# Two accumulating chains in PSUM instead of a separate addition per product, neighbouring sets interleaved, and no split weight unit kept in DRAM

## The chip, the cores and the metric

The kernel runs on one core of one Trainium2 chip. The metric is the time of one execution in microseconds (us), as the device measures it. Five engines work side by side, each through its own queue of instructions in order: TensorE (PE in the profile, with its weight loads as PEld), VectorE (DVE), ScalarE (ACT), GpSimd (POOL, unused here) and SyncE (SP, which issues all DMAs). TensorE writes its results to PSUM, which has eight banks; DVE and ACT read them from there.

## The reference, cut to what matters

```
scores = 1/sqrt(64) * q @ k.T - log(448)            # 4 batches, 12 heads, 448 rows, head size 64
x = (sigmoid(scores) @ v), heads side by side       # [1792, 768]
h = x @ w_in;  g = s * relu(h)**2 + b;  x = g @ w_out          # layer 0: 768 -> 2048 -> 768
h = x @ w_in2; g = max(h,0) + alpha * min(h,0); out = g @ w_out2   # layer 1, the same sizes
```

All is in float32. The weights arrive as 64-bit floats and are made into 32-bit ones on the chip.

## The kernel before, in words

**Attention** comes first: 84 units of QK products, a sigmoid on ACT, and products with V. **Then eight phases** follow, each 504 matmuls: layer 0 and layer 1 (m), each in two halves of the tokens (g), each half an "in" phase (times w_in) and an "out" phase (times w_out). The order is in(m,g), out(m,g) for (0,0), (0,1), (1,0), (1,1).

**Seven products.** Each phase multiplies 2x2 blocks with seven products M1 to M7 in place of eight. The sums of weight blocks that they need (S1 to S4) are made by `quad`, which loads 64-bit weights (tile `r`), turns them into 32-bit ones on ACT (line 303) and DVE (306, 311), forms the sums (324) and stores seven blocks to DRAM (`w0in`, `w0out`, `w1in`, `w1out`; line 342). A phase later reads these back in units of eight 128x128 blocks into `raw` (two buffers).

**Splits.** Each float32 operand is split into a high and a low part: ACT casts (line 397), DVE subtracts (line 400). Weight units go to `ring` (three buffers; in the first phase `rinq`, four smaller buffers over the same memory, filled straight from `quad`'s blocks), the "in" operand to `xo`, the "out" operand to `gb`. One weight block costs three matmuls (lines 491 to 493).

**In phase.** Eight sets (`mp`), one after the other. A product is 9 matmuls, a set 63. The results of a set are four blocks of `g`, which then go through the nonlinearity (lines 534, 535, 538 in layer 0; 553, 555, 558 in layer 1). `IN_ORDER` sets the order in a set. M1 is copied from its bank by ACT (502); M5, M6, M7, M4 and M3 are each added to a sum in SBUF by DVE (512, 520); M2 goes on top of M1 in M1's bank and is copied.

**Out phase.** Seven products one after the other, each for three output parts `k` with 24 matmuls each (one weight unit). The additions are made in the same way, and results are stored by SP (617). While a product runs, `prepare` makes the operand of the next one; under the last product the next phase's operand is loaded and split as well.

**Kept units.** In out(0,0) the split units from number `FROM` = 10 on (11 of 21) are stored to DRAM (`s0out`), and out(0,1) loads them instead of splitting them again.

**Order of the instructions.** All work is recorded in `Plan`, with an estimated duration each. `Plan.place` then fixes each engine's order: the PE keeps its recorded order, and every other engine takes the work that could start first, and of equals the most urgent one. The chip runs the queues so made; the estimates only set the order.

Of the kernel before, what the change touches and what calls it, by code (L numbers as in the profile page):

```python
# [16 lines left out]
P = 128  # L17
# [4 lines left out]
ROUNDS = 3  # L22
EARLY = 7
FROM = 10
# [5 lines left out]
IN_ORDER = ["M1", "M5", "M6", "M2", "M4", "M7", "M3"]  # L30
OUT_ORDER = ["M1", "M5", "M2", "M6", "M7", "M4", "M3"]
LEFT = {"M1": "A11", "M2": "A12", "M3": "S4", "M4": "A22", "M5": "S1", "M6": "S2", "M7": "S3"}
CHUNKS = [(0, 3), (3, 6), (6, 8)]


class Plan:
# [25 lines left out]
    def order(self):  # L62
# [10 lines left out]
        for _ in range(ROUNDS):  # L73
            late = [0.0] * n
            for i in range(n - 1, -1, -1):
                dur, lat = self.ops[i][1:3]
                x = min((late[s] for s in succ[i]), default=t + 50) - dur - lat
                late[i] = min(x, goal[i]) if i in goal else x
            done, at = self.place(succ, late, list(goal))
            goal = {i: at[i] for i in goal}  # L80
        return done

    def place(self, succ, late, pe):
# [10 lines left out]
        while len(done) < n:  # L94
# [29 lines left out]
            for s in succ[i]:  # L124
                est[s] = max(est[s], end + (lat if self.ops[s][0] != eng else 0.0))
# [30 lines left out]
def tile_kernel(  # L156
# [83 lines left out]
    ps = psp.tile([P, 8, 512], F32, name="ps")  # L240

# [3 lines left out]
    def act_t(n, psum=False):  # L245
        return (0.146 if psum else 0.183) + 0.844e-3 * n

    def dve_t(n, psum=False):
        return 0.155 + 1.037e-3 * n

    def dve2_t(n):
        return 0.16 + 0.53e-3 * n
# [23 lines left out]
    def quad(m, kind, k, c, place=0):  # L276

        QUAD = QUADS[place]
        order = IN_ORDER if kind == "in" else OUT_ORDER
# [53 lines left out]
        if kind == "in":  # L333
            dst = d[:, 7 * k * WQ : 7 * (k + 1) * WQ]
            src = sb(QUAD, 7 * n)
            wrote = [("d", m, kind, 7 * KH * k + i) for i in range(7 * KH)]
        else:
            dst = d.rearrange("p (i m n) -> p i m n", i=7, m=NDP)[:, :, k, c0 * P : c1 * P]
            src = q
            wrote = [("d", m, kind, (i * NDP + k) * 8 + j) for i in range(7) for j in range(c0, c1)]  # L340
        add(
            "SP", dma_t(7 * n), lambda: nc.sync.dma_start(out=dst, in_=src),
# [11 lines left out]
    def entry(at, n, ring_=RING):  # L354
        dst = ring_[n_unit[0] % len(ring_)]
        n_unit[0] += 1
        for j in range(n // P):
            ring[at // P + j] = (dst + j * P, dst + (n + j * P))
        return dst

    def unit(m, kind, i, g):
        at, n = i * UNIT, UNIT
        dst = entry(at, n)
# [23 lines left out]
    def direct(mp, place):  # L387

        for b0, b1 in ((0, 2), (2, 4), (4, 6), (6, 7)):
            n = (b1 - b0) * WQ  # L390
            dst = entry((7 * mp + b0) * WQ, n, RING4)
            split(dst, dst + n, QUADS[place] + b0 * WQ, n)
            yield
# [48 lines left out]
    def make_x(par, raw):  # L442
# [6 lines left out]
        def less(o, x, y):  # L449

            for t, a, e in x if len(x) > 1 else y:
# [10 lines left out]
        less(p[0], p[0], p[2])  # L462
# [63 lines left out]
    def nonlinear(m, par, mp, ps_):  # L526
# [4 lines left out]
        if m == 0:  # L531
            n = len(ps_) * S
            h, c = at(ps_)
            add("ACT", act_t(n), lambda: nc.scalar.activation(h, h, AF.Relu), c, c)
            add("ACT", act_t(n), lambda: nc.scalar.activation(h, h, AF.Square), c, c)
            add(
                "ACT", act_t(n) + 0.19,
                lambda: nc.scalar.activation(h, h, AF.Identity, bias=b_t, scale=s_t),
                c + [("sc",)] + [("bc",)], c,
            )  # L540
            return
        for row in range(2):
            some = [p for p in ps_ if p // 2 == row]
            if not some:
                continue
            n = len(some) * S
            h, c = at(some)
            ct = cells(NEG, n)
            t = sb(NEG, n).rearrange("p (b n) -> p b n", n=S)
# [3 lines left out]
                lambda t=t, h=h: nc.scalar.activation(t, h, AF.Relu, scale=-1.0), c, ct,  # L553
            )
            add("ACT", act_t(n), lambda h=h: nc.scalar.activation(h, h, AF.Relu), c, c)
# [7 lines left out]

    def in_phase(m, g, par):
        made = 0
        get = None
        for mp in range(NMP):
            k0 = 4 * (mp % 2)
            a, c, bb, e = k0, k0 + 1, k0 + 2, k0 + 3
            to = {"M1": a, "M2": a, "M5": c, "M4": c, "M6": bb, "M7": bb, "M3": e}  # L570
            second = {"M2", "M4", "M7"}
            if m == g == 0:
                get = direct(mp, 1 - mp % 2)
            for i, x in enumerate(IN_ORDER):
                terms = []
                for kc in range(KH):
                    n = (mp * 7 + i) * KH + kc
                    while (m or g) and made <= n // 8:
                        unit(m, "in", made, g)
                        made += 1  # L580
                    if m == g == 0 and i % 2 == 0 and kc == 0:
                        next(get)
                    xo = X[par][i]
                    terms.append((*ring[n], xo + kc * S, xo + XB + kc * S))
                mm_group(to[x], terms, x not in second, True, x in second)
                if x == "M1":
                    t = tmp()
                    pcopy(t, a)
                elif x == "M5":
                    s_ = tmp()  # L590
                    padd(s_, c, t)
                    free(t)
                elif x == "M6":
                    q = tmp()
                    padd(q, bb, s_)
                elif x == "M2":
# [344 lines left out]
```

## Time and profile before

| | us |
|---|---|
| three runs, median (lowest to highest) | 975.98 (974.36 to 978.29) |
| the profiled execution's own time | 972.68 |
| its span, first to last instruction | 970.9 |
| PE busy / DVE busy / ACT busy | 954.9 / 761.7 / 619.4 |

The profiled execution lies 3.3 us below the median. A busy PE is no proof of a full pace, since matmul records overlap; a stall shows as a longer step from one matmul's start to the next.

### The profile page before, as it was taken

Reading aid. Unit: us, or ns where it says so; the run is one execution under the profiler, and the core shown is the slowest. Engines: PE = TensorE matmul, PEld = TensorE weight load, DVE = VectorE, ACT = ScalarE, POOL = GpSimd, SP = SyncE. Lnnn points to the kernel's source line nnn. Section 1 sums busy time; section 2 is a strip of 40 time slices with the busy share of each in tenths; the row PEclk is TensorE's granted clock in tenths of the full one; section 3 lists DMA queues with packets and bytes.
Section 4 is the critical chain, followed back from the end, with each engine's and each line's share of the span. In section 5 each row is a group of like instructions: output and inputs, shape, how many; then the busy total and the mean of one; then the engine's idle time right before and its main releaser. Section 6 shows DMA issues by size and latency. Waiting matters only on the chain. (4 is left out here: it accounts for less than half of the span.)

```text
span 970.9 us, 13854 instructions
## 1 busy us (share of the span) xinstructions
PE 954.9 (98%) x5424; PEld 815.0 (84%) x5424; DVE 761.7 (78%) x905; ACT 619.4 (64%) x678; POOL 0.2 (0%) x4
## 2 busy tenths in 40 slices
PE   9999999998999999999999999997999999999998
PEld 4334459997999999999999999997999999999997
DVE  3547678888987987889988788989989666689862
ACT  7989966779864557879644366667545455576440
POOL 0000000000000000000000000000000000000000
PEclk9999999999999999999999999998999999999999
DMA  9999986685559998897489987775544443333441
GB/s 325 368 330 340 336 302 257 224 298 199 161 166 390 338 337 303 310 352 249 139 306 353 353 297 258 250 235 190 161 127 155 127 119 104 110 102 109 141 145 66
DMA packets 69618, 228.98 MB, mean 236 GB/s; under 512 B 6577, under 2 KB 30897, under 8 KB 64689
## 3 DMA queue, kind: packets, MB, share of 16 engines
q1 hardware_dynamic: 69552, 228.10, 67.9%
q8 instruction: 42, 0.69, 0.3%
q14 instruction: 24, 0.19, 0.0%
HBM read 158.74 MB, written 69.34 MB: 235 GB/s over the span
## 5 line engine op out<-in xcount | busy, mean ns | idle before, releaser
L491 PE MATMUL ps<-gb,ring 128*128 128x448 f32 x672 | 247.4, 368 | 6.8 <-DVE gb L400 5.2
L493 PE MATMUL ps<-gb,ring 128*128 128x448 f32 x672 | 247.0, 368 | 1.7 <-DVE ring L400 1.7
L492 PE MATMUL ps<-gb,ring 128*128 128x448 f32 x672 | 246.9, 367 | 0.0
L397 ACT CAST ring<-raw 128x1024 fp32r<-128x1024 f32 x136 | 142.3, 1048 | 147.1 <-PE ps L492 120.6
L400 DVE TENSOR_TENSOR ring<-raw,ring 128x1024 fp32r<-128x1024 f32 x136 | 165.7, 1220 | 24.0 <-ACT ring L397 23.4
L491 PE MATMUL ps<-xo,ring 128*128 128x448 f32 x504 | 184.1, 365 | 0.0
L493 PE MATMUL ps<-xo,ring 128*128 128x448 f32 x504 | 184.1, 365 | 0.0
L492 PE MATMUL ps<-xo,ring 128*128 128x448 f32 x504 | 184.1, 365 | 0.0
L491 PEld LDWEIGHTS ps<-gb,ring 128*128 128x128 f32 x672 | 127.3, 189 | 18.5 <-DVE gb L400 6.6
L493 PEld LDWEIGHTS ps<-gb,ring 128*128 128x128 f32 x672 | 127.2, 189 | 12.3 <-DVE ring L400 2.0
L492 PEld LDWEIGHTS ps<-gb,ring 128*128 128x128 f32 x672 | 127.2, 189 | 10.1
L400 DVE TENSOR_TENSOR gb<-g,gb 128x1344 fp32r<-128x1344 f32 (+1 forms) x84 | 116.8, 1398 | 15.9 <-ACT gb L397 9.1
L512 DVE TENSOR_TENSOR tmp<-ps,tmp 128x448 f32<-128x448 f32 x124 | 76.8, 622 | 61.2 <-PE ps L493 47.8
L397 ACT CAST gb<-g 128x1344 fp32r<-128x1344 f32 (+1 forms) x84 | 99.5, 1191 | 34.7 <-PE ps L493 29.7
L493 PEld LDWEIGHTS ps<-xo,ring 128*128 128x128 f32 x504 | 94.7, 188 | 7.5
L491 PEld LDWEIGHTS ps<-xo,ring 128*128 128x128 f32 x504 | 94.7, 188 | 7.5
L492 PEld LDWEIGHTS ps<-xo,ring 128*128 128x128 f32 x504 | 94.7, 188 | 7.5
L767 ACT ACTIVATE sg<-ps,bias 128x896 f32<-128x896 f32 x84 | 82.8, 1010 | 11.5 <-PE ps L751 11.0
L751 PE MATMUL ps<-kq 64*64 64x448 f32 x672 | 81.8, 541 | 2.6 <-ACT sg L767 2.5
L789 PE MATMUL ps<-sg,v 64*64 64x448 f32 x672 | 81.9, 536 | 0.0
L303 ACT ACTIVATE r<-r 128x768 f32<-128x768 f32 (+1 forms) x68 | 59.0, 875 | 29.7 <-DMA r<-in_w_out 14.0
L410 DVE TENSOR_TENSOR g<-g 128x1344 f32<-128x1344 f32 (+1 forms) x48 | 66.4, 1396 | 0.2
(49 smaller groups left out, 985.7 us busy)
## 6 DMA issues: line engine op xcount, KB each, us to landing
r<-in_w_in SPq DMA_DIRECT2D x32, 768.0 KB, 5.7
raw<-w1in SPq DMA_DIRECT2D x42, 512.0 KB, 3.6
raw<-w1out SPq DMA_DIRECT2D x42, 512.0 KB, 3.5
r<-in_w_out SPq DMA_DIRECT2D x24, 768.0 KB, 6.0
raw<-w0out SPq DMA_DIRECT2D x31, 512.0 KB, 3.8
s0out<-ring SPq DMA_DIRECT2D x11, 1024.0 KB, 8.0
ring<-s0out SPq DMA_DIRECT2D x11, 1024.0 KB, 7.7
raw<-w0in SPq DMA_DIRECT2D x21, 512.0 KB, 4.8
```

The lines of the kernel that those rows point to most:

```text
L303: nc.scalar.activation(hi, hi, AF.Prelu, scale=2.0**-112, alpha=-(2.0**32))
L397: add("ACT", act_t(n), lambda: nc.scalar.copy(h, x), cells(src, n), cells(hi, n))
L400: lambda: nc.vector.tensor_tensor(out=l, in0=x, in1=h.bitcast(F32), op=ALU.subtract),
L410: lambda: nc.vector.tensor_tensor(out=o_, in0=x_, in1=y_, op=ALU.subtract),
L491: nc.tensor.matmul(d, wh_, ml_, start=first and k == 0, stop=False, **opt)
L492: nc.tensor.matmul(d, wh_, mh_, start=False, stop=False, **opt)
L493: nc.tensor.matmul(d, wl_, mh_, start=False, stop=last and k == n, **opt)
L512: lambda: nc.vector.tensor_tensor(out=d, in0=bank(k), in1=o, op=ALU.add),
L751: nc.tensor.matmul(ps[h * D : (h + 1) * D, k + j, :S], a.ap[rows, S + k0 : S + k0 + D], a.ap[rows, :S], start=True, stop=True,)
L767: lambda: nc.scalar.activation(o, i, AF.Sigmoid, bias=sb(BIAS, 1), scale=QKSCALE),
L789: nc.tensor.matmul(ps[j * D : (j + 1) * D, k + h, :S], va[keys, v : v + D], a.ap[keys, j * S : (j + 1) * S], start=first, stop=last,)
```

## The change

- **Two chains in PSUM.** M1, M6, M7 and M4 are summed in one bank one on top of the other (block sums are taken with such signs that all are added); M5 and M3 in a second bank; M2 stands alone. ACT copies the first chain after M1, M6 and M7, and in an in phase the last state goes through the nonlinearity straight from PSUM. DVE makes three additions per set where it made five. A product of the chain can start only when ACT has copied the state before it.
- **Sets interleaved.** In the in phases the products of neighbouring sets are mixed (`in_order`): M1 of the next set comes before M3 of this one, and the last two sets end with M4, M4, M3, M3. `quad` stores its blocks for an in phase in several pieces, as they now stand in that order (48 DMAs in all, before 16).
- **No unit kept.** `FROM` = 21: nothing is stored to or loaded from `s0out`; out(0,1) splits all of its 21 units.
- **Ring.** After the first in phase the count that picks the `ring` buffer is set to 0.
- **Planner's estimates.** Each ACT or DVE duration is 0.08 or 0.09 us shorter, and a dependent instruction must wait that much more (`PIPE`).

```diff
+PIPE = {"DVE": 0.08, "ACT": 0.09}
-FROM = 10
+FROM = 21
-IN_ORDER = ["M1", "M5", "M6", "M2", "M4", "M7", "M3"]
-OUT_ORDER = ["M1", "M5", "M2", "M6", "M7", "M4", "M3"]
+OUT_ORDER = ["M1", "M5", "M2", "M6", "M7", "M3", "M4"]
+def in_order(n):
+    seq = []
+    for k in range(n - 1):
+        seq += [("M1", 0)] if k == 0 else []
+        seq += [(x, k) for x in (("M5", "M6", "M2", "M7") if k == 0 else ("M6", "M5", "M7", "M2"))]
+        if k + 2 < n:
+            seq += [(x, k) for x in (() if k == 0 else ("M4",))] + [("M1", k + 1)]
+            seq += [(x, k) for x in (("M4", "M3") if k == 0 else ("M3",))]
+    seq += [(x, n - 1) for x in ("M1", "M2", "M6", "M5", "M7")]
+    return seq + [(x, k) for x in ("M4", "M3") for k in (n - 2, n - 1)]
...
     def act_t(n, psum=False):
-        return (0.146 if psum else 0.183) + 0.844e-3 * n
+        return (0.056 if psum else 0.093) + 0.844e-3 * n
...
+        for i, (x, mp) in enumerate(SEQ):
+            a, c, b = ((3, 2, 1), (5, 4, 0))[mp % 2]
+            to = {"M5": c, "M3": c, "M2": b}.get(x, a)
+            more = x in ("M6", "M7", "M4", "M3")
...
+            mm_group(to, terms, not more, True, more)
...
+            if x == "M1":
+                pcopy(p1, a)
+            elif x == "M6":
+                pcopy(p2, a)
+            elif x == "M2":
+                padd(p1, b, p1)
...
+            elif x == "M7":
+                pcopy(p4, a)
+                padd(p4, c, p4)
...
+            elif x == "M4":
+                nonlinear(m, par, mp, [2], a)
...
+            elif x == "M3":
+                padd(p2, c, p2)
...
             "M1": (P1, None), "M5": (P1, (P2, P1)), "M2": (P3, None), "M6": (P1, (P4, P1)),
-            "M7": (P2, (P4, P2)), "M4": (P1, (P1, P3)), "M3": (P4, None),
+            "M7": (P2, (P4, P2)), "M4": (P1, (P3, P1)), "M3": (P4, None),
...
+                bk = {"M2": 6 + k % 2, "M5": 3 + k, "M3": 3 + k}.get(x, k)
+                more = x in ("M6", "M7", "M4", "M3")
...
         if n == 0:
+            n_unit[0] = 0
             produce(Q1)
```

How this moves the instructions is shown at three places, all on ACT. In the rows `g` is the in phase's result, `ps` is PSUM, L534 is the copy of a chain's state, L536, L570, L605 and L608 are the parts of layer 0's nonlinearity, L429 the cast of a split and L322 `quad`'s conversion (before: L502, L534, L535, L538, L397, L303).

Place 1 is the second set of in(0,0). Of the kernel before, from the copy of M1 to that of M1+M2 and the square behind it:

```order
L502 COPY tmp_82<-ps 128x448
L397 CAST rinq_63<-quadb 128x768
L303 ACTIVATE r_76<-r_76 128x768
L534 ACTIVATE g_115<-g_115 128x4x448
L303 ACTIVATE r_77<-r_77 128x768
L397 CAST rinq_64<-quadb 128x768
L502 COPY g_115<-ps 128x448
L535 ACTIVATE g_115<-g_115 128x4x448
```

Of the change, from the nonlinearity of the set before (first M4 from PSUM, then the two blocks that M3 ends) to the copy behind this set's M7:

```order
L536 ACTIVATE g_115<-ps 128x448
L429 CAST rinq_63<-quada 128x384
L570 ACTIVATE g_115<-g_115 128x2x448
L605 ACTIVATE g_115<-g_115 128x4x448
L534 COPY g_115<-ps 128x448
L429 CAST rinq_66<-quadb 128x768
L322 ACTIVATE r_76<-r_76 128x768
L608 ACTIVATE g_115<-g_115,bc,sc 128x4x448
L534 COPY g_115<-ps 128x448
```

There are now copies after M6 and after M7, and the first of the two stands behind the square (L605) of the set before.

Place 2 is the end of in(0,0). Of the kernel before, up to the first weight units of out(0,0):

```order
L502 COPY g_115<-ps 128x448
L534 ACTIVATE g_115<-g_115 128x448
L538 ACTIVATE g_115<-g_115,bc,sc 128x4x448
L397 CAST ring_62<-raw_67 128x1024
L535 ACTIVATE g_115<-g_115 128x448
L538 ACTIVATE g_115<-g_115,bc,sc 128x448
L397 CAST gb_119<-g_115 128x896
L397 CAST ring_60<-raw_68 128x1024
```

Of the change, from the copy behind the last set's M6; the next copy is that behind its M7:

```order
L534 COPY g_115<-ps 128x448
L608 ACTIVATE g_115<-g_115,bc,sc 128x448
L570 ACTIVATE g_115<-g_115 128x448
L429 CAST ring_60<-raw_67 128x1024
L429 CAST gb_118<-g_115 128x1344
L534 COPY g_115<-ps 128x448
L605 ACTIVATE g_115<-g_115 128x448
L429 CAST gb_120<-g_115 128x1344
L608 ACTIVATE g_115<-g_115,bc,sc 128x448
L536 ACTIVATE g_115<-ps 128x448
```

The first unit's cast, into ring 60 and no longer ring 62, has moved from behind the phase's last product to the end of M7 with four products to follow, and it and a cast to `gb` stand ahead of the copy behind M7.

Place 3 is the last conversion of 64-bit weights (for `w1out`) in in(1,0). Of the kernel before, beginning with the first cast to `gb`, the operand of out(1,0):

```order
L397 CAST gb_117<-g_115 128x1344
L397 CAST ring_62<-raw_68 128x1024
L303 ACTIVATE r_76<-r_76 128x512
L303 ACTIVATE r_77<-r_77 128x512
L553 ACTIVATE neg<-g_115 128x896
```

Of the change, the last two such conversions; ten unit casts follow them before the first cast to `gb`:

```order
L534 COPY g_115<-ps 128x448
L590 ACTIVATE g_115<-g_115 128x2x448
L322 ACTIVATE r_76<-r_76 128x512
L429 CAST ring_62<-raw_67 128x1024
L588 ACTIVATE neg<-g_115 128x448
L322 ACTIVATE r_77<-r_77 128x512
```

The conversions have moved from beside the first casts to `gb`, at the end of in(1,0), to ten weight units ahead of them (a unit is 24 matmuls, as a product's part in an out phase).

## Rows read from the trace of the kernel before

**Rows 1.** The page's span and PE's line.

```profile
span 970.9 us, 13854 instructions
PE   954.9 (98%) x5424; PEld 815.0 (84%) x5424; DVE 761.7 (78%) x905; ACT 619.4 (64%) x678; POOL 0.2 (0%) x4
```

**Rows 2.** Busy time by stretch: attention, all eight phases, out(0,1).

```profile
core 0: us, PE busy (x) PEld busy (x) DVE busy (x) ACT busy (x) POOL busy (x), PEclk, DMA share, GB/s
0.00:136.00 136.00, 132.31 (x1393) 55.44 (x1394) 77.10 (x112) 116.41 (x139) 0.20 (x4) 1.00 0.93 331
136.00:967.40 831.40, 822.63 (x4032) 759.56 (x4032) 684.00 (x793) 503.00 (x539) 0.00 (x0) 0.99 0.64 221
455.00:555.00 100.00, 100.00 (x496) 92.57 (x495) 85.54 (x88) 48.69 (x51) 0.00 (x0) 1.00 0.80 279
```

**Rows 3.** PE in order of time, undisturbed: first and last of 190 matmuls.

```profile
699.66 0.37 PE L493 MATMUL ps<-gb,ring 128*128 128x448 f32 x1
...
737.97 0.36 PE L493 MATMUL ps<-gb,ring 128*128 128x448 f32 x1
```

**Rows 4.** PE in order of time, end of in(0,0) and begin of out(0,0).

```profile
238.42 0.37 PE L493 MATMUL ps<-xo,rinq 128*128 128x448 f32 x1
240.07 0.47 PE L491 MATMUL ps<-gb,ring 128*128 128x448 f32 x1 [1.28 <-ACT ring L397]
...
242.40 0.47 PE L493 MATMUL ps<-gb,ring 128*128 128x448 f32 x1 [1.66 <-DVE ring L400]
...
243.47 0.57 PE L491 MATMUL ps<-gb,ring 128*128 128x448 f32 x1
...
246.70 0.36 PE L491 MATMUL ps<-gb,ring 128*128 128x448 f32 x1
```

**Rows 5.** ACT and DVE there: the split of the first unit.

```profile
238.99 1.03 ACT L397 CAST ring<-raw 128x1024 fp32r<-128x1024 f32 x1
...
241.14 1.22 DVE L400 TENSOR_TENSOR ring<-raw,ring 128x1024 fp32r<-128x1024 f32 x1
```

**Rows 6.** PE in order of time, end of in(1,0) and begin of out(1,0).

```profile
653.90 0.37 PE L493 MATMUL ps<-gb,ring 128*128 128x448 f32 x1
...
654.70 0.37 PE L492 MATMUL ps<-gb,ring 128*128 128x448 f32 x1
...
656.13 0.37 PE L493 MATMUL ps<-gb,ring 128*128 128x448 f32 x1
661.75 0.74 PE L491 MATMUL ps<-gb,ring 128*128 128x448 f32 x1 [5.25 <-DVE gb L400]
...
666.39 0.36 PE L491 MATMUL ps<-gb,ring 128*128 128x448 f32 x1
```

**Rows 7.** ACT, SP and DVE there, in order of time on each.

```profile
644.13 1.23 ACT L303 ACTIVATE r<-r 128x512 f32<-128x512 f32 x2
...
653.55 1.05 ACT L397 CAST ring<-raw 128x1024 fp32r<-128x1024 f32 x1 [4.73 <-DMA raw<-w1out]
...
648.53 0.33 SPq L268 DMA_DIRECT2D raw<-w1out  x1
...
660.61 1.08 DVE L400 TENSOR_TENSOR gb<-g,gb 128x896 fp32r<-128x896 f32 x1
```

**Rows 8.** Groups of instructions by line and shape: busy us, mean ns of one.

```profile
L397 ACT CAST gb<-g 128x1344 fp32r<-128x1344 f32 x56 | 73.6, 1316 | 31.7 <-PE ps L493 29.7 <-DVE xo L400 1.9
...
L512 DVE TENSOR_TENSOR g<-ps,tmp 128x448 f32<-128x448 f32 x64 | 39.6, 620 | 17.3 <-PE ps L493 17.1
...
L535 ACT ACTIVATE g<-g 128x1792 f32<-128x1792 f32 x14 | 23.8, 1700 | 0.0
...
L502 ACT COPY g<-ps 128x448 f32<-128x448 f32 x32 | 16.8, 524 | 6.1 <-PE ps L493 5.9
...
L534 ACT ACTIVATE g<-g 128x896 f32<-128x896 f32 x2 | 1.9, 941 | 0.0
```

**Rows 9.** Who waited for whom: PE's two longest of six, ACT's for weights.

```profile
PE ps L491 <- DVE gb L400: 5.2, 1, 5.2
PE ps L751 <- ACT sg L767: 2.5, 6, 0.8
...
ACT r L303 <- DMA r<-in_w_out: 14.0, 14, 3.5
...
ACT r L303 <- DMA r<-in_w_in: 9.6, 11, 1.6
```

More of the change, by code (lines that the diff above doesn't have):

```diff
@@ L240, in tile_kernel @@
     ps = psp.tile([P, 8, 512], F32, name="ps")
+    SEQ = in_order(NMP)
+    TURN = {x: i for i, x in enumerate(SEQ)}
+    ROWS = [[x for x, k in SEQ if k == mp] for mp in range(NMP)]
     plan = Plan()
@@ L278, in quad @@
         QUAD = QUADS[place]
-        order = IN_ORDER if kind == "in" else OUT_ORDER
+        order = ROWS[k] if kind == "in" else OUT_ORDER
         pos = {LEFT[x]: i for i, x in enumerate(order)}
@@ L449, in less @@
         def less(o, x, y):
-            for t, a, e in x if len(x) > 1 else y:
+            for t, a, e in x:
                 n = e - a
@@ L461, in make_x @@
         half(3, p[2])
-        less(p[0], p[0], p[2])
+        less(p[0], p[2], p[0])
         half(4, p[0])
@@ L531, in nonlinear @@
         if m == 0:
[L532 to L540, printed above, removed]
+            if bank_ is not None:
+                (p,) = ps_
+                pcopy(g_place(par, p, mp), bank_, AF.Relu)
+            else:
+                n = len(ps_) * S
+                h, c = at(ps_)
+                add("ACT", act_t(n), lambda: nc.scalar.activation(h, h, AF.Relu), c, c)
             return
@@ L562, in nonlinear, with scaled @@
             )
+    def scaled(m, par, mp, ps_):
+        if m == 0:
+            n = len(ps_) * S
+            h = g_blocks(par, ps_, mp)
+            c = [c for p in ps_ for c in cells(g_place(par, p, mp), S)]
+            add("ACT", act_t(n), lambda: nc.scalar.activation(h, h, AF.Square), c, c)
+            add(
+                "ACT", act_t(n) + 0.19,
+                lambda: nc.scalar.activation(h, h, AF.Identity, bias=b_t, scale=s_t),
+                c + [("sc",)] + [("bc",)], c,
+            )
@@ L564, in in_phase @@
     def in_phase(m, g, par):
         made = 0
[L566 to L596, printed above, removed]
-                    pcopy(g_place(par, 0, mp), a)
-                    if mp == NMP - 1:
-                        nonlinear(m, par, mp, [0])
-                elif x == "M7":
-                    padd(g_place(par, 3, mp), bb, s_)
-                    free(s_)
-                    psub(g_place(par, 2, mp), g_place(par, 3, mp), c)
-                    if mp == NMP - 1:
-                        nonlinear(m, par, mp, [2, 3])
-                elif x == "M3":
-                    padd(g_place(par, 1, mp), e, q)
-                    free(q)
-            nonlinear(m, par, mp, [1] if mp == NMP - 1 else [0, 1, 2, 3])
-            if m == 0 and g == 0 and mp + 2 < NMP:
-                if mp % 2 == 1 and EARLY + mp // 2 < len(outs):
-                    quad(*outs[EARLY + mp // 2])
-                quad(m, "in", mp + 2, 0, 1 - mp % 2)
@@ L662, in out_phase @@
                     ]
-                    mm_group(to[x][k], terms, x not in second and j0 == 0, j1 == 8, x in second)
-                bk = to[x][k]
+                    mm_group(bk, terms, not more and j0 == 0, j1 == 8, more)
                 if x == "M1":
```

139 lines of the change are left out of this document (91 added, 48 removed).

## The prediction

> **What bounds the kernel now.** The page shows PE busy for 954.9 of 970.9 us [rows 1]; the question is where PE steps slower than it could. Read first the pace: 189 steps from one matmul's start to the next take 38.31 us, 0.2027 us each, where nothing disturbs [rows 3]. The eight phases hold 4032 matmuls [rows 2], 817.3 us at that pace, and take 831.4. So 14.1 us are lost there, and nothing that only makes DVE or ACT lighter can give more than that. Next, where they are lost, by the order of time on PE at the two phase ends with the longest waits.
>
> At the end of in(0,0) the matmul of 238.42 is followed 16 steps later by that of 246.70 [rows 4]: 8.28 us for 3.24, a loss of 5.0. Two waits lie in it. The first unit of out(0,0) goes into ring 62, over the `rinq` buffer that the last product still reads; so its cast can begin only at 238.99, behind that product, and its low part, behind other DVE work, at 241.14 [rows 5]. Then PE steps in 0.37 us in place of 0.20 until 246.46: behind the two pauses it runs at the lower of its two clock levels.
>
> At the end of in(1,0) the matmul of 656.13 is followed 13 steps later by that of 666.39 [rows 6]: 10.26 us for 2.64, a loss of 7.6, and just ahead two steps from 653.90 take 0.80 for 0.41. What is late is no arithmetic of the phase. ACT sat 4.73 us before a unit's cast, for data of `w1out` that was asked for at 648.53, since the last conversions of those weights ran at 644.13 [rows 7]. Behind that cast, in ACT's queue, stood the last sets' nonlinearity, and behind that the low part of `gb` at 660.61 for which PE waited. Both places together cost 13.0 us; the remaining 1.1 lies in short pauses.
>
> **The change, part by part.** *Ring and interleaving, end of in(0,0).* The first unit's buffer is now one that the last two products do not read. By place 2 of the order, its cast stands behind M7 with four products to go, 36 x 0.2027 = 7.3 us ahead of need; cast 1.03 and low part 1.22 [rows 5] fit. The 5.0 us go, with one new wait in their place: the second M4 needs the copy behind the last M7, and ahead of that copy stand the unit's cast, 1.03, and a `gb` cast, 1.32 [rows 8]. With 0.52 for the copy, less 0.1 for each of two overlaps and plus 0.1 for both hand-overs (238.99 + 1.03 against 240.07 leaves 0.05 for one), that is 2.8 us after M7 where M4 is due after 1.8: 1.0 us. Net gain 4.0.
>
> *Planner and lighter DVE, end of in(1,0).* By place 3 the last conversions stand ten units earlier, 10 x 24 x 0.2027 = 49 us. The wait for data was 4.73, so nothing near it is left. I take all of 8.0 (7.6 + 0.4). DVE has room for this since five additions per set become three: 8 sets of an in phase save 16 x 0.62 = 9.9 us [rows 8].
>
> *Chains.* In a set, M1 to M6, M6 to M7 and M7 to M4 now each wait for a copy by ACT, with one to two products of 1.82 us between. A copy of 0.52 and two hand-overs of 0.05 leave 1.2 us in which ACT may be busy with something else. The casts (1.03) fit into that; the square of 1.70 [rows 8] does not always. Place 1, from the end of M3 (t = 0): addition 0.05 + 0.62, nonlinearity 0.05 + 0.94, square 1.70 from about 1.7, copy from 3.3 to 3.85, and M7 due at 3.65 after M6 and M5: 0.2 us late. The pattern stands twice in the 14 interleaved sets of layer 0: 0.4 us. Layer 1 has no such long instruction.
>
> The other thing that can stand ahead of a copy is an ACT instruction that waits for 64-bit weights: 25 times, 23.6 us in all, the longest 3.5 [rows 9]. Only what exceeds 1.2 us, and stands right ahead of a copy, reaches PE. From nothing (in 25 waits of 0.94 on average) to 4 us (two or three of the longest kind); I take 1.5, nearer to the mean.
>
> *Units no longer kept.* out(0,1) splits 11 units more: 11 x 1.22 = 13.4 us on DVE and 11 x 1.03 on ACT, hidden under PE. DVE was busy 85.5 of 100 us there [rows 2]; six additions less in each out phase take off 3.7, so some 95 of 100, by records that overlap by 0.1 each. It fits; without that cover DVE would be the bound and the surplus show, up to 5 us if the two weight conversions that the order also brings there come on top. I take 0. The DMAs lose 11 stores and 11 loads of 1 MB and gain 11 loads of half that, in a phase where the queues were busy 0.80 [rows 2]; the 32 extra pieces of `quad`'s stores cost SP 0.3 to 0.5 us each, spread over 500 us, against loads that are asked for units ahead. 0.
>
> *Attention.* Its code is the same, but the planner's estimates shift ACT's order. PE's busy time lacks 3.7 us there [rows 2], 2.5 of it waits for the sigmoid [rows 9]. The order may take these away or double them: 0, with bounds of 2.5 to either side.
>
> *The last instruction* is a copy of 0.52 in place of an addition of 0.62: -0.1.
>
> **The sum**: -5.0 + 1.0 - 8.0 + 0.4 + 1.5 - 0.1 = -10.2 us. Against the profile's own 972.68 us that is 962.5. That execution lies 3.3 below the median of the runs, so on their scale 975.98 - 10.2 = **965.8 us**. Under about 0.5% (4.9 us) a change here cannot be told from none.
>
> **The rivals.** *The copies wait after all (the other side).* The place is each set's three hand-overs between PE and ACT. Before, a chain had only M1 to M2, with two products between, and PE's list of waits, six rows, has no copy [rows 9]. Now ACT has about 50 more of them and its longest instructions are unchanged. With 32 sets, 13.0 / 32 = 0.41 us of PE waiting per set eats all the gain, and 0.56 us makes it slower by 0.5%. Half of the break-even (6.5 us in place of my 1.9) gives 970.4; all of it 975.9; with a drop of the clock behind such waits, at 0.17 us a step for some ten steps as in [rows 4], ten drops would add 17 and give over 980. Against it: my walk gives 0.2 us in two sets of 14, and 1.0 once.
>
> The Trainium skill, "PSUM — Partial Sum Buffer", in its summary of rules for kernel authors, says to read a PSUM bank while matmuls write a different one. The chain goes against this by itself: it reads a bank and then accumulates on it. If no other product stood between, each of 96 copies would cost PE its 0.52 and two hand-overs, 0.62 in all, some 60 us, and the time would be near 1025; the order puts M3, M5 or M2, in other banks, between, and no row of before shows the tight case.
>
> *The late weights stay late.* If w1out is again the last thing that arrives, by DMA load rather than order, only the ring's part stays: -5.0 + 2.8 = -2.2, so 973.8. For it: ACT's waits for 64-bit weights, 14.0 us for w_out alone [rows 9]. Against it: 49 us of lead.
>
> *More than forecast.* No new waits at all, and the 1.1 us and attention's 2.5 go too: -16.7, so 959.3.
>
> **How the numbers follow.** Forecast (stalls gone, new waits of 1 to 6 us): 0.66. More: 0.10. Copies eat half to all: 0.12, of which 0.06 is within 0.5%. Late weights: 0.07. Slower through the copies or through DVE in out(0,1): 0.05. Faster by over 0.5%, below 971.1: 0.66 + 0.10 + 0.06 = 0.82; within: 0.06 + 0.07 = 0.13; slower: 0.05. The range goes from the case with everything gone, 959, a little lower for attention, 958, to 972, where 5.9 us of new waits more than forecast and all lesser cases are in.
>
> **What the profile after would show.** Right: PE's start-to-start steps stay at 0.20 over both phase ends, with one pause near 1 us in the last products of in(0,0), and no lower clock at out(1,0); the last conversions for w1out near 600 us; DVE lighter by some 40 us (88 additions of 0.62 less, 13.4 more). Wrong: PE waits for L534 in sums of many us in in(0,0) and in(0,1); a clock below full in a slice of an in phase; DVE at 100 of 100 in out(0,1) with PE waiting for `ring`; an attention that ends later than 136 us by more than 2.5.

## The result, and the profile after

The change made the kernel slower. 20 executions of it have a median of 984.22 us (978.23 to 993.76), 20 of the kernel before on the same chips 977.31 (970.46 to 985.98). The ratio is 1.0059, with a 95% interval of 1.0038 to 1.0081; the slowest execution, 993.76, lies over 1.5% above the fastest and is left out of it. Forecast were 965.8 us, 958 to 972.

The profiled execution took 982.76 us (before: 972.68). Of the page, the span and PE's line, which answer to [rows 1]:

```profile
span 981.0 us, 13850 instructions
PE 958.9 (98%) x5424; PEld 809.8 (83%) x5424; DVE 723.1 (74%) x846; ACT 660.5 (67%) x821; POOL 0.2 (0%) x4
```

Busy time by stretch, as [rows 2]: attention, the eight phases, out(0,1).

```profile
0.00:137.20 137.20, 132.16 (x1392) 51.98 (x1392) 73.62 (x109) 116.02 (x138) 0.20 (x4) 1.00 0.91 322
137.20:977.50 840.30, 826.55 (x4036) 757.86 (x4032) 649.47 (x738) 543.93 (x682) 0.00 (x0) 1.00 0.60 199
457.00:557.00 100.00, 100.00 (x495) 92.70 (x494) 95.34 (x97) 63.91 (x74) 0.00 (x0) 1.00 0.68 226
```

DVE has lost 35 us in the phases and ACT has gained 41. Neither is full, and yet the phases are 8.9 us longer. The two places that were late before are mended. PE in order of time at the end of in(0,0) (as [rows 4]), and at the begin of out(1,0) (as [rows 6]):

```profile
242.93 0.37 PE L525 MATMUL ps<-xo,rinq 128*128 128x448 f32 x1
244.25 0.47 PE L523 MATMUL ps<-xo,rinq 128*128 128x448 f32 x1 [0.96 <-ACT g L534]
...
667.98 0.36 PE L525 MATMUL ps<-xo,ring 128*128 128x448 f32 x1
668.18 0.36 PE L523 MATMUL ps<-gb,ring 128*128 128x448 f32 x1
...
687.77 0.47 PE L523 MATMUL ps<-gb,ring 128*128 128x448 f32 x1 [1.19 <-DVE gb L432]
```

The 5.0 us at the first place are 1.2 now (1.32 + 0.31 for two steps of 0.20), of which 0.96 is the wait for a copy that was forecast as 1.0. At the second, PE goes on without a pause; a wait of 1.19 follows 20 us later, and another like it in out(1,1). The loss is in PE's list of waits, which had no copy before [rows 9]:

```profile
PE ps L523 <- ACT g L534: 9.0, 11, 3.8
PE ps L795 <- ACT sg L811: 3.9, 8, 1.2
PE ps L523 <- DVE gb L432: 2.4, 2, 1.2
PE ps L523 <- ACT tmp L534: 2.3, 1, 2.3
```

PE waits 12 times, 11.3 us, for a copy (L534), all of it in the in phases (the 2.3 at 563.83 for the last copy of out(0,1), whose bank in(1,0) needs, so that it is no link of a chain; ACT stood 2.59 us ahead of it for weights). Three more places show what stands ahead of the copy; with that one they make 7.9 of the 11.3 us. First the longest, PE, ACT and SP near 219 us:

```profile
219.07 0.37 PE L525 MATMUL ps<-xo,rinq 128*128 128x448 f32 x1
223.21 0.48 PE L523 MATMUL ps<-xo,rinq 128*128 128x448 f32 x1 [3.77 <-ACT g L534]
...
227.53 0.36 PE L524 MATMUL ps<-xo,rinq 128*128 128x448 f32 x1
...
221.89 0.83 ACT L429 CAST rinq<-quadb 128x768 fp32r<-128x768 f32 x1 [5.09 <-DMA raw<-w0out]
222.63 0.53 ACT L534 COPY g<-ps 128x448 f32<-128x448 f32 x1
...
217.29 0.32 SPq L287 DMA_DIRECT2D raw<-w0out  x1
```

From 219.07 to 227.53 PE makes 14 steps, 8.46 us in place of 2.84: 5.6 lost. The copy is ready to run but stands behind a cast that waits 5.09 us for a load of out(0,0)'s first weight unit. The cast does not use that load. It reads `quadb`; but the two `raw` buffers lie over the same memory, and the load was put ahead of the last reads of `quadb`, so the read waits until it has landed. The kernel before has this wait too, on DVE, ahead of its last read of `quadb` (SP and DVE):

```profile
215.09 0.33 SPq L268 DMA_DIRECT2D raw<-w0out  x1
...
218.91 0.56 DVE L400 TENSOR_TENSOR rinq<-quadb,rinq 128x384 fp32r<-128x384 f32 x1 [2.46 <-ACT rinq L397]
```

The cast that this row names had ended at 213.65; the load landed at 218.79. It cost nothing there, as PE makes no pause between 201 and 238 us. After the pause of the change PE steps in 0.37 for ten steps; the granted clock there was 0.51, the lower of its two levels, and 1.00 behind it:

```profile
223.90:227.20 3.30, 3.30 (x10) 2.94 (x10) 2.59 (x5) 2.95 (x5) 0.00 (x0) 0.51 0.69 222
227.50:242.00 14.50, 14.50 (x73) 13.43 (x73) 11.62 (x14) 11.73 (x17) 0.00 (x0) 1.00 0.43 169
```

The other two, ACT near 352 us (PE loses 1.0) and near 620 us (1.3):

```profile
352.05 0.92 ACT L322 ACTIVATE r<-r 128x768 f32<-128x768 f32 x1 [3.47 <-DMA r<-in_w_in]
...
355.15 0.93 ACT L322 ACTIVATE r<-r 128x768 f32<-128x768 f32 x1 [0.82 <-DMA r<-in_w_in]
355.96 0.53 ACT L534 COPY g<-ps 128x448 f32<-128x448 f32 x1
...
620.06 0.95 ACT L588 ACTIVATE neg<-g 128x896 f32<-128x896 f32 x1 [3.57 <-DVE g L544]
621.05 0.95 ACT L590 ACTIVATE g<-g 128x896 f32<-128x896 f32 x1
621.90 0.51 ACT L534 COPY g<-ps 128x448 f32<-128x448 f32 x1
```

Once it is a conversion whose weights have not landed, once the nonlinearity of the set before, put into the queue before DVE's last addition is done. In all three ACT had been idle, not busy.

**All runs in one table.** Of PE's steps in the eight phases, those of 0.215 us or more are taken as pauses, the rest as pace, each by what it exceeds 0.2027; a step counts for the phase in which it begins. With the begin of the first phase this accounts for the time: own time less these three is 822.4 to 823.2 us in every profile. The medians are of 6 to 20 executions, the ratios against 17 to 29 executions of the kernel before on the same chip (the change: 20); medians of different chips are not compared here, ratios are. Names are those of the experiments below.

| kernel | first phase at | pauses | pace | own time | median | ratio (95%) |
|---|---|---|---|---|---|---|
| before | 135.9 | 14.1 | 0.0 | 972.68 | 977.31 | 1 |
| the change | 137.2 | 22.1 | 1.0 | 982.76 | 984.22 | 1.0059 (1.0038 to 1.0081) |
| e1_whole_quadb | 140.3 | 16.2 | 4.9 | 984.62 | 984.42 | 1.0061 (1.0028 to 1.0094) |
| e2_conv_later | 135.1 | 24.9 | 9.2 | 991.64 | 990.34 | 1.0119 (1.0066 to 1.0171) |
| e3_both | 135.2 | 26.6 | 4.8 | 989.06 | 987.6 | 1.0095 (1.006 to 1.0129) |
| e4_before_ring | 135.7 | 11.5 | 2.9 | 972.76 | 976.11 | 0.9973 (0.9937 to 1.001) |
| f1_before_estimates | 134.7 | 17.3 | 1.9 | 976.59 | 981.52 | 1.0013 (0.9982 to 1.0044) |
| f2_after_old_estimates | 141.2 | 8.1 | 0.2 | 971.93 | 978.08 | 1.0002 (0.997 to 1.0034) |
| f3_dve_copy | 136.7 | 17.2 | 4.2 | 980.74 | 984.31 | 1.0057 (1.0021 to 1.0094) |
| g1_pairs | 142.0 | 63.5 | 1.2 | 1029.37 | 1029.56 | 1.052 (1.0474 to 1.0566) |
| h1_attention_later | 134.1 | 16.1 | 1.8 | 974.44 | 974.25 | 0.999 (0.9957 to 1.0022) |
| h2_keep_units | 139.7 | 10.8 | 5.8 | 979.04 | 982.7 | 1.0058 (1.0028 to 1.0088) |
| h3_no_reset | 139.6 | 13.7 | 4.4 | 980.62 | 981.4 | 1.0062 (1.0031 to 1.0093) |
| h4_copies_twice | 140.6 | 24.1 | 5.9 | 993.1 | 993.02 | 1.0174 (1.0133 to 1.0215) |
| j1_after_first_in_tmp | 137.3 | 18.1 | 9.5 | 988.1 | 984.81 | 1.0063 (1.0029 to 1.0097) |
| j2_old_estimates_first | 138.5 | 4.1 | 7.0 | 972.03 | 970.29 | 0.9903 (0.9865 to 0.9941) |
| j3_attention_first | 134.6 | 6.4 | 0.7 | 964.53 | 968.85 | 0.9885 (0.9845 to 0.9924) |
| k1_durations_only | 141.3 | 28.0 | 9.7 | 1001.52 | 994.2 | 1.0149 (1.0102 to 1.0196) |
| k2_pipe_only | 136.8 | 19.2 | 6.2 | 984.7 | 981.36 | 1.0017 (0.9981 to 1.0052) |
| k3_dma_slower | 135.9 | 20.2 | 1.6 | 980.14 | 981.5 | 1.0016 (0.9987 to 1.0045) |

Two columns are partly chance. Pace goes from 0 to 9.7 us (see the last section). The first phase begins at 137.2, 140.3 and 136.7 in three profiles in which attention's order is the same (the change, e1, f3). Each kernel has one profile only, and that execution can lie off its median (f2's 6.2 us below, k1's 7.3 above). So pauses are compared by profile, and times only by the ratios with their intervals.

### The profile page after: what moved, and what is told of

It reads as the page before. It is cut to its first block, busy times and chain, and to the rows that moved or that the text cites. A ratio compares the mean times of both kernels' runs of the same rounds, so it can differ in the third digit from the quotient of the medians.

```text
span 981.0 us, 13850 instructions
## 1 busy us (share of the span) xinstructions
PE 958.9 (98%) x5424; PEld 809.8 (83%) x5424; DVE 723.1 (74%) x846; ACT 660.5 (67%) x821; POOL 0.2 (0%) x4
## 4 chain that ended last, share of the span: by engine, by line
PE 69%; DVE 11%; DMA 9%; ACT 8%; issue 2%; DVEq 0%; ACTq 0%
PE ps L523 22%; PE ps L525 21%; PE ps L524 21%; DMA r<-in_w_out 4%; DMA w0out<-quada 4%; PE ps L795 2%; PE ps L833 2%; DVE quada L330 2%; DVE ring L432 1%; DVE xo L432 1%; ACT sg L811 1%; DVE quada L343 1%; DVE quada L325 1%; ACT r L322 1%; ACT g L534 1%
## 5 line engine op out<-in xcount | busy, mean ns | idle before, releaser
L429 ACT CAST ring<-raw 128x1024 fp32r<-128x1024 f32 x147 | 154.3, 1050 | 116.1 <-PE ps L524 104.0
L432 DVE TENSOR_TENSOR ring<-raw,ring 128x1024 fp32r<-128x1024 f32 x147 | 179.5, 1221 | 69.7 <-ACT ring L429 69.4
L432 DVE TENSOR_TENSOR gb<-g,gb 128x1344 fp32r<-128x1344 f32 (+1 forms) x84 | 116.2, 1398 | 18.6 <-ACT gb L429 16.1
L429 ACT CAST gb<-g 128x1344 fp32r<-128x1344 f32 (+1 forms) x84 | 99.7, 1193 | 21.1 <-PE ps L525 15.9
L795 PE MATMUL ps<-kq 64*64 64x448 f32 x672 | 79.3, 546 | 4.0 <-ACT sg L811 3.9
L833 PE MATMUL ps<-sg,v 64*64 64x448 f32 x672 | 77.8, 536 | 0.0
L322 ACT ACTIVATE r<-r 128x768 f32<-128x768 f32 (+1 forms) x68 | 58.9, 876 | 26.4 <-DMA r<-in_w_out 17.7
L544 DVE TENSOR_TENSOR g<-ps,g 128x448 f32<-128x448 f32 x96 | 58.6, 620 | 21.9 <-ACT g L534 10.2
L534 ACT COPY g<-ps 128x448 f32<-128x448 f32 x96 | 50.4, 525 | 33.1 <-PE ps L525 32.3
```

Source lines behind the costliest of these rows:

```text
L322: nc.scalar.activation(hi, hi, AF.Prelu, scale=2.0**-112, alpha=-(2.0**32))
L429: add("ACT", act_t(n), lambda: nc.scalar.copy(h, x), cells(src, n), cells(hi, n))
L432: lambda: nc.vector.tensor_tensor(out=l, in0=x, in1=h.bitcast(F32), op=ALU.subtract),
L534: nc.scalar.copy(d, bank(k))
L544: lambda: nc.vector.tensor_tensor(out=d, in0=bank(k), in1=o, op=ALU.add),
L795: nc.tensor.matmul(ps[h * D : (h + 1) * D, k + j, :S], a.ap[rows, S + k0 : S + k0 + D], a.ap[rows, :S], start=True, stop=True,)
```

## The experiments

**Is it the load ahead of the copy?** e1 makes the planner see the shared memory:

```diff
-            [("d", m, kind, 8 * i + j) for j in range(8)], cells(raw, n),
+            [("d", m, kind, 8 * i + j) for j in range(8)],
+            cells(QUADS[1], 7 * WQ) if (m, kind, g) == (0, "out", 0) and i < 2 else cells(raw, n),
```

> The changed kernel, with one dependency more for the planner: the first two loads of w0out units into raw are said to write all of the buffer quadb whose memory they share, so they are placed behind the last cast that reads quadb. Theory A (ACT's queue stands on a DMA landing ahead of a chain's copy): the pause of PE at 219 us in the profile of the change (3.9 us, two slow hand-overs, ten steps at 0.37 in place of 0.20, 5.9 us in all) goes and nothing takes its place; the time falls by about 6 us against the change, so the ratio to the kernel before goes from 1.006 to about 1.000. Rival B (the chains' copies are late by themselves, since ACT has too much to do between two products): a pause of 2 us or more comes back at this place behind a copy, now with ACT busy and not waiting ahead of it, and the time falls by less than 2 us.

The pause at 219 us went, and pauses fell by 5.9 us; but the time did not. Part of the gain was given back at once: the first load now comes after the last set's reads, at 241.81, and out(0,0) waits for it. PE there:

```profile
247.92 0.47 PE L524 MATMUL ps<-gb,ring 128*128 128x448 f32 x1 [2.62 <-ACT ring L430]
249.40 0.74 PE L526 MATMUL ps<-gb,ring 128*128 128x448 f32 x1 [0.81 <-DVE ring L433]
```

In the profile the rest went into a later first phase and a slower pace. So the wait is what makes the pause, as theory A says; the time is rival B's, whose pause of 2 us or more did not come.

e2 has the planner take weights to land 3 us later (`DMA_LAT + 3.0` for the loads of `r`), e3 both:

> The changed kernel, where the planner takes each load of 64-bit weights to land 3 us later, so that ACT's conversions of them are put further back in its queue; nothing else is edited, but the order on all engines but PE may shift with it. Theory A: the pause at 561 us (2.5 us, a slow hand-over and ten steps at 0.37, 4.3 us in all) goes, ACT's waits for 64-bit weights fall from 26 us to under 10 and their longest under 1.5; since the first load of a w0out unit also comes to stand behind the cast that waited for it at 219 us, that pause of 5.9 us goes too: some 10 us less than the change, a ratio of 0.995 to 0.997 to the kernel before. Rival B: the pauses come back behind copies with ACT busy ahead of them, and the time falls by less than 3 us.

> The edits of the two kernels above together. Theory A: no pause of PE over 1.5 us in the in phases, the time as with the later conversions alone or up to 1 us under it. Rival B: as above, less than 3 us under the change.

Theory A is refuted as a remedy. ACT's waits for 64-bit weights fell from 26.2 to 5.3 us in e2 and in in(1,0) the pauses from 6.5 to 1.5, as expected, but in in(0,0) pauses rose from 10.1 to 19.4 (e3: 16.3): there each set's weights are converted just ahead of their use, and conversions put back made casts late (PE waits 4.9 us at 207 us in e2 and 4.7 at 209 in e3, each for a cast of `rinq`). The load over `quadb` held e2 up as well: DVE waits 4.03 us for it, and PE, behind that, 3.12 for a copy at 233 us. So one margin does not fit all phases.

**The ring alone.** e4 is the kernel before with `n_unit[0] = 0` behind in(0,0):

> The kernel before, with the change's one line that sets the count of the ring to 0 after the first in phase, and nothing else of the change. If the pause at the end of in(0,0) was the ring's (the prediction's step): the 5.0 us go and the ratio is 0.994 to 0.996. Rival: something else in the kernel before is late there (the unit's data, or the operand gb), then a pause of over 1.5 us stays there and the ratio is above 0.998.

Pauses of in(0,0) and out(0,0) fell from 5.7 to 3.8 us, not to zero: at 246.41 PE then waits 3.15 us for `gb` (L400), which the ring's pause had covered. The ratio does not differ from 1.

**Estimates or chains?** f1 is the kernel before with the change's estimates, f2 the change with the old ones:

```diff
-PIPE = {"DVE": 0.08, "ACT": 0.09}
+PIPE = {}
-        return (0.056 if psum else 0.093) + 0.844e-3 * n
+        return (0.146 if psum else 0.183) + 0.844e-3 * n
```

(and the two of DVE likewise).

> The kernel before with the change's shorter estimates of the planner and its PIPE, and nothing else: no chain, no interleaving, units kept, the ring as before. By its order the last conversions for w1out stand at product 36 of in(1,0) (before: 50, the change: 24). Theory C (the estimates alone mended the late w1out): the pause behind in(1,0), 8.0 us before, falls under 2 us, while the pause at the end of in(0,0), 5.0 us, stays: ratio 0.993 to 0.995. Rival D (only a DVE with fewer additions lets them come early enough): over 5 us are left of the pause, ratio 0.997 to 1.002.

> The changed kernel with the estimates of the kernel before: chains, interleaving, the ring and no unit kept stay. Theory E (the chains' copies in a queue that ACT shares with loads, casts and long nonlinearities are what lost the time): PE's waits for copies stay, over 6 us in sum in in(0,0) to in(1,0), and the ratio stays at or above 1.004. Rival F (the order that came of the new estimates, which put a load ahead of the reads of quadb and a conversion ahead of copies, lost it): waits for copies under 3 us and a ratio of 0.997 or less.

f1: the pause behind in(1,0) went from 8.1 to 1.1 us (theory C), but other pauses came, 7.0 in in(0,0) for 2.1 and 6.0 in out(0,1) for none; no gain. f2: pauses fell from the change's 22.1 to 8.1 us and the ratio from 1.0059 to 1.0002. Chains, interleaving and copies are all still there, so most of the loss came with the new order, as F says. Its ratio of 0.997 and its waits under 3 us were missed: copies are still waited for, 4.6 us, and in this profile attention ended late (141.2). The longest pause is again near the place of the change's. DVE and ACT in f2:

```profile
222.50 0.96 DVE L432 TENSOR_TENSOR rinq<-quadb,rinq 128x768 fp32r<-128x768 f32 x1 [5.29 <-DMA raw<-w0out]
223.38 0.55 DVE L343 TENSOR_TENSOR quada<-quada 128x384 f32<-128x384 f32 x1
...
224.30 0.83 ACT L429 CAST rinq<-quada 128x768 fp32r<-128x768 f32 x1 [3.49 <-DVE quada L343]
...
226.35 0.51 ACT L534 COPY g<-ps 128x448 f32<-128x448 f32 x1
```

Now DVE's low part is the read of `quadb` that waits for the load; ACT waits for DVE, and the copy for ACT.

**Another engine for the copies.** f3 makes the in phases' 96 copies on DVE (`nc.vector.tensor_copy`):

> The changed kernel, with the three copies of each set's chain in the in phases made by DVE and not by ACT; the out phases stay. Theory E: ACT's queue, whose instructions ahead of a copy wait for loads or take 1.7 us and more, is what makes copies late; DVE's instructions are shorter (0.6 to 1.8 us) but some wait for ACT in turn, so the sum of PE's waits for copies falls from 11 us to under 6 and the time falls by 3 to 8 us against the change. Rival G (a copy between two products of one chain is late on whichever engine makes it, since both are over 75% busy in in(0,0)): the waits for copies stay over 9 us in sum and the time within 3 us of the change or above it.

Waits for these copies are 6.5 us (6 times; 9.0 in the change), between the two theories, and the ratio is that of the change: G by the time. The longest, 4.18 us at 220.62, is the same load: ACT's cast waits 4.09 us for it, DVE's low part waits for the cast, and the copy stands behind that.

**More products between copy and need.** g1 runs two sets in step in in(0,1), (1,0) and (1,1):

```diff
+def pair_order(n):
+    return [
+        (x, j) for k in range(0, n, 2) for x in ("M1", "M5", "M6", "M2", "M7", "M3", "M4") for j in (k, k + 1)
+    ]
```

> The changed kernel, in whose in phases (0,1), (1,0) and (1,1) two sets go in step (M1 of both, M5 of both, and so on), so that three products, 5.5 us, stand between a copy and the product that needs it, where one or two did, 1.8 us and up; in(0,0) keeps its order, and its pauses. Theory E: the pauses of in(0,1) and in(1,0), 3.3 and 6.5 us in the profile of the change, go to under 1 us each; in(0,0) keeps about 10; some 8 us less than the change, ratio about 0.998. Rival G' (what is late in these phases is the weights' or operands' way and not the slack of the copy): as many us of pauses are left, behind DVE or casts, and the time is within 3 us of the change.

No copy of a chain is waited for in these three phases any more, as E expects. But the time says nothing of either theory, since the order brought dearer waits of its own. In in(0,1) PE waits four times, 3.8 us, for additions on DVE. In layer 1 the next pair's M1 needs a bank that the nonlinearity still reads behind M4. PE waits for it six times, 4.1 to 6.4 us each; at 605.28 for the first, whose ACT line is

```profile
604.68 0.54 ACT L594 ACTIVATE neg<-ps 128x448 f32<-128x448 f32 x1 [0.75 <-DVE g L599]
```

**Four edits of f2.** h1 puts attention's conversions 3 us back, h2 sets `FROM = 10`, h3 leaves `n_unit[0] = 0` out, h4 makes each copy twice:

```diff
+                pcopy(p1, a, again=True)
...
+                pcopy(p2, a, again=True)
...
+                pcopy(p4, a, again=True)
```

> The changed kernel with the old estimates, and besides, for the loads of 64-bit weights that are recorded before the first in phase, the planner takes a landing 3 us later. Theory H (attention's length is set by where these conversions stand in ACT's queue, since they wait there for loads ahead of a sigmoid; its profile with the old estimates alone showed attention's end at 141.2 us, the one with all conversions taken later at 135.1): attention ends at 135 to 136.5, the pauses of the eight phases stay at 8 to 9 us, and the ratio to the kernel before is 0.993 to 0.996. Rival I (attention's end varies by some 5 us from run to run whatever its order): the time is within 2 us of the kernel with old estimates, ratio 0.998 to 1.002.

Attention's sigmoid waits went, the first phase begins 7.1 us sooner, and in(0,0) still ends at 250.4 (f2: 249.9): its pauses rose from 6.3 to 14.2. Half of theory H fell; what attention gains is lost again as long as something later holds in(0,0).

> The changed kernel with the old estimates, with 11 split units of out(0,0) kept in DRAM again (FROM = 10). The prediction's step (splitting them again is hidden): no difference over 2 us, ratio 0.998 to 1.002. Rival J (the loads of kept units, 1 MB each, come late near the end of out(0,1), as a wait of 1.8 us for s0out showed in the kernel before with new estimates): a wait for s0out of 1 to 2 us with steps at the lower clock, 2 to 6 us slower, ratio 1.002 to 1.006.

Kept units bring no speed, and the wait for `s0out` is 0.31 us. What this profile has more than f2's is a wait of 2.99 us for `gb` at 683.23 (4.8 with what follows), and pace. Neither theory named this.

> The changed kernel with the old estimates, without the line that sets the count of the ring to 0, so that out(0,0) begins with the buffer over the rinq that the last products read. The prediction's step (the ring made a pause of 5.0 us, in whose place one of 1.0 stands): 4 to 5 us of pauses more at the end of in(0,0), ratio 1.004 to 1.005. Rival K (with M4, M4, M3, M3 at the end of the phase the last reader of that buffer is early enough, or another wait stands there anyway): under 2 us, ratio under 1.002.

The prediction's step holds within the change: at the begin of out(0,0) stand waits of 2.21 and 0.67 us, with what follows 6.2 us of pauses, where f2 has none; in(0,0) up to there has 1.5 less, mostly the wait of 0.96 in the last products. The 4.7 us more lie in the 4 to 5 expected; the ratio rises by 0.0060, some 5.9 us.

> The changed kernel with the old estimates, in which each copy of a chain's state in the in phases (96 of 0.52 us) is made twice, the second one free of cost in the planner's eyes, so that all orders stay as they are. The prediction's step (1.2 us of slack around a copy, which only long instructions or waits ahead of it use up): most of the second copies, 0.42 us each on ACT, are hidden, the pauses grow by 0 to 4 us, mostly in in(0,0), and the ratio stays under 1.005. Rival G (a copy has no slack worth speaking of): 96 x 0.42, some 40 us more, ratio about 1.04.

Between the two: pauses grew by 16.0 us and the ratio by 0.0172, some 17 us. That is 0.17 us of pauses for each of 96 second copies of 0.42. Waits for copies went from 4 to 22:

```profile
PE ps L523 <- ACT g L534: 14.7, 22, 2.6
```

Most copies have slack for 0.42 us more (74 of 96 are not waited for), but not all have 1.2.

**The load off that memory, and early.** j1 (on the change), j2 (on f2) and j3 (on h1) load the first unit into the temporaries' memory, unused in an in phase, and the next two behind all reads of `quadb`:

```diff
+    RAWT = tensor("rawt", TMP[4].base, UNIT)
...
+        early = i if (m, kind, g) == (0, "out", 0) else 9
+        raw = RAWT if early == 0 else RAW[n_unit[1] % NRAW]
+        n_unit[1] += early > 0
...
+            cells(QUADS[1], 7 * WQ) if early in (1, 2) else cells(raw, n),
```

> The changed kernel; the first w0out unit of out(0,0) is loaded into memory of the temporaries, unused in an in phase, and the next two loads are placed behind all reads of quadb. No read of quadb waits for a load any more, and the first unit is there early. Theory L (that wait makes the pause at 219 us): pauses of in(0,0) fall from 10.5 us to 4 or 5 with no new one at the begin of out(0,0); the time falls by 5 to 6 us against the change, ratio 0.999 to 1.001. Rival M (in(0,0) cannot end earlier, since loads and conversions of w_in set its pace; the first attempt, and attention made 7 us shorter, both gave their gain back): the pause goes but others grow, out(0,0) begins at 248 to 250 us as before, ratio 1.004 to 1.007.

> The same edit in the changed kernel with the old estimates. Theory L: its pause of 2.9 us behind a copy in in(0,0), with the steps at the lower clock 4.6 us, goes: ratio 0.994 to 0.997. Rival M: out(0,0) begins at 248 to 250 us as with the old estimates alone, ratio 0.998 to 1.002.

> The same edit in the kernel with old estimates and attention's conversions taken 3 us later. Theory L: the pause behind a copy near 227 us (4.1 us, with the lower clock 5.9) goes, out(0,0) begins near 244 us, ratio 0.992 to 0.995, a version that beats both kernels. Rival M: it begins at 248 to 250 us again, ratio 0.997 to 1.001.

With the old estimates theory L holds: the pause is gone, pauses are 4.1 and 6.4 us, and both kernels beat the kernel before by more than L expected, j3 by 1.15%, with out(0,0) from 241.1 us. For j3 pauses account for the gain (9.7 us less than h1's, the ratio lower by 0.0105); for j2 they don't: its ratio is 0.0099 under f2's, with only 4.0 us less of pauses from one profile to the other (f2's execution lies 6.2 us under its median). PE's waits in j3, where the copy's longest is 0.9:

```profile
PE ps L528 <- ACT g L539: 3.1, 6, 0.9
...
PE ps L800 <- ACT sg L816: 1.0, 1, 1.0
...
PE ps L530 <- DVE ring L437: 0.2, 1, 0.2
```

On the change itself (j1) in(0,0) lost 4.8 us of its pauses, 4.6 came up in out(0,0), where the second and third unit were late, and the time stayed: rival M's time, by another way than it said.

**Which of the estimates?** k1 is j1 with `PIPE = {}`, k2 j1 with the old durations, k3 j1 with `DMA_LAT = 3.4`:

> The kernel with the first unit in the temporaries' memory and the new, shorter durations, but no PIPE. Theory N (shorter durations let the planner put conversions, whose loads come later than it thinks, ahead of copies): waits for weights ahead of copies as with both new estimates, last w1out conversion near product 24 of in(1,0), ratio 1.003 to 1.008. Rival O (PIPE does it, by ranking dependent instructions otherwise): ratio 0.988 to 0.995.

> The same with the old durations and PIPE. Its last w1out conversion stands near product 40 of in(1,0), as with the old estimates. Theory N: ratio 0.988 to 0.995, as with the old estimates (0.990). Rival O: ratio 1.003 to 1.008.

> The same with both new estimates, and every DMA taken to land 1.2 us later (DMA_LAT 3.4 for 2.2). Theory N: fewer waits for loads ahead of copies, PE's pauses in the in phases fall by a third or more against the kernel without this edit, ratio 0.995 to 1.001. Rival: conversions and quads come later in in(0,0) than the products need them, as in the run with all conversions 3 us later, and the ratio is 1.006 or more.

Neither N nor O: the durations alone are worse than both together (1.0149), PIPE alone costs too (1.0017, against 0.9903 with neither), and later landings may help a little (1.0016 against 1.0063, with intervals that overlap). In k3 pauses of in(0,1) and in(1,0) fell from 5.8 to 2.0 us and those of in(0,0) rose from 5.3 to 13.0, as in e2. That the estimates cost the time is shown; by which rule they do is not.

## Why the prediction was wrong

- **What bounds the kernel, and the two stalls:** right. The ring's pause went with one of 0.96 us in its place (1.0 forecast), and without the reset (h3) 6.2 us came back at the begin of out(0,0), 4.7 net. In the kernel before, the reset alone (e4) uncovers a wait for `gb` there and gains less.
- **The late weights:** right in effect (8.0 forecast, 8.1 to 1.5), since the last conversions ran at 593.96 and 596.75 and not at 644. The reason given, room on DVE, is not needed: with the new estimates the old additions do it as well (f1, 1.1 left), and with the old estimates the lighter DVE does (f2, none left).
- **The step that failed: "Chains", and in it "Only what exceeds 1.2 us, and stands right ahead of a copy, reaches PE ... I take 1.5".** The copies were to cost 0.4 + 1.5 + 1.0 = 2.9 us; the in phases' pauses in the change are 19.3 (10.1, 2.7, 6.5), 17.7 of them at or right behind a wait for a copy. Three things were missed. The instruction ahead of a copy may wait not only for 64-bit weights, but for any load or for DVE, as at 219 and 620 us. A load can be made to matter to a reader by shared memory alone: that it stands ahead of the last reads of `quadb` could be seen in SP's order before the run, and in the trace of the kernel before in a wait of 2.46 us on DVE that no product felt, and the text looked at ACT's order only. And each of the two longest pauses, at 219 and 561 us, brings some ten steps at the lower clock, about 1.6 us, which the text priced only among the rivals. Its bound for this term, 4 us, was built from single waits of 3.5 us in a kernel in which nothing urgent stood behind them.
- **"A copy leaves 1.2 us":** too generous; h4 shows 0.17 us of each further 0.42 exposed. The Trainium skill, "PSUM — Partial Sum Buffer", in its rules for kernel authors, wants PSUM read while matmuls write another bank. The prediction said that a chain goes against this; the order keeps to it, as a product in another bank runs while a chain's bank is read. The 60 us worked out for a chain with nothing between did not come, and no run here has that case.
- **Planner's estimates:** costed only for attention and the last conversions. With the old ones the same chains run at 1.0002 (f2), with the shared memory mended at 0.9903 (j2) against 1.0063 (j1), some 15.6 us, more than any term of the sum.
- **Units not kept:** 0, right: DVE is busy 95.34 of 100 in out(0,1), as forecast, and PE does not wait there; keeping them was no gain (h2).
- **Attention:** 0 within 2.5. In three profiles with the change's order it ends 0.8 to 4.4 us later than before.
- **The rivals:** "The copies wait after all" is what happened, at the time of its dearest case (over 980), but by 11.3 us of waits and two drops of the clock in place of ten. Its case "all of it 975.9" leaves out the pause of 1.0 that the case before it counts; counted alike it is 976.9. It had 0.12 and a part of 0.05, too little: the walk behind it asked whether ACT is busy, not whether it waits.

Profile against profile the 10.1 us are: attention +1.4, pauses +8.0, pace +1.0, the end -0.3. By the medians it is 6.9.

Open is why the ratio of j1 is not below that of the change with 4 us less of pauses (its profile has 8.5 us more of pace), and what in the estimates makes the order bad. Not separated either are the chains and the interleaving: no run has the one without the other.

## What to carry to other kernels

Before a result that was read once becomes a link that the next product needs, look not at how busy the reading engine is but at what stands ahead of each such read in its queue and what that waits for: loads, other engines, and buffers over the same memory. Look at the order of the queue that issues loads as well, above all where a load moves across the last read of memory that it shares. And when planner estimates change, time them apart: here they decided between 1% faster and 0.6% slower with the same arithmetic.

## What the runs showed of the hardware beside that

Undisturbed matmuls of one shape have two paces. [rows 3] show 0.2027 us; in j2 in(1,1) has 504 steps from 760.04 to 864.20, 0.2067 each, with a granted clock of 1.00. First, next-to-last and the window of j2:

```profile
760.04 0.37 PE L526 MATMUL ps<-xo,ring 128*128 128x448 f32 x1
...
863.99 0.37 PE L528 MATMUL ps<-xo,ring 128*128 128x448 f32 x1
864.20 0.37 PE L526 MATMUL ps<-gb,ring 128*128 128x448 f32 x1
...
760.10:864.10 104.00, 104.00 (x505) 94.45 (x504) 60.62 (x69) 66.03 (x96) 0.00 (x0) 1.00 0.35 104
```

It costs 2.0 us in a phase, can hold for longer than that (in e1 from 256 to 359 us, in j2 from 623 to 883), and is found in the kernel before too, with the ring's reset (e4, from 135.7 to 200.3 us and from 882.9 on). The one profile of before has none of it, which may be part of why its 972.68 us lie under the median. For comparison, the Trainium skill, "TensorE: Matmul & The Clock Gate", section "Back-to-back issue gap", gives N/2.4 + 2.5 ns for the gap of an isolated matmul, an estimate of 189 ns for 448 columns; both paces here are above it. What chooses between the two is open. In e1 the change from the first to the second, at 256 us, stands behind two steps of 0.30 and 0.31, and in the profile of the change all eight changes of pace, either way, stand behind one or two steps of 0.24 to 0.40.
